# A long convolution and an MLP on one core: k transposed by DMA, q's statistics from an early copy, shorter tables, h transposed by DMA

## The chip, the cores and the metric

The kernel runs on one core of a Trainium2 chip. The metric is the device time of one execution in microseconds. The kernel before was run three times: 261.87, 262.96 and 264.95 us, so its median is 262.96 us.

## The reference

All arrays are bf16. q, k and v are 2048 x 512 (time by channel), and the filter `ssm_k` is 512 x 2048. F is 1792.

```
k_shift[s] = sum over j in 0..3 of k[s - j] * shift_k[:, j]        # four taps, zeros before the start
kv = k_shift * v
y  = irfft(rfft(kv, 4096) * rfft(ssm_k, 4096))[:2048] + kv * ssm_D   # causal convolution along time
h  = q + layernorm(q) * y
x  = layernorm(h)                                                    # the block below works on this
g  = gelu(layernorm(x) @ w1)
g  = its four channel groups shifted by -1, +1, -2, +2 time steps
x1 = x + g @ w2
out = h + x1 + gelu(layernorm(x1) @ w3) @ w4
```

## The kernel before

The long convolution is computed as a two-level Fourier transform by matmuls. A time index s is split as s = 32 n1 + n2 with n1 below 64. The k part first applies the four taps, multiplies by v and gets `kv`; the rows of `kv` then have to lie with n1 on the partitions, and so do the rows of the filter h (`Rk` and `Rh`). A first level of matmuls (`stage_a`, 16 calls for k and 16 for h) gives `Tk` and `Th`; a second (`stage_c`, 16 calls for each) gives the spectra `xt`; DVE multiplies them (`product`); two more levels go back (L647 and `last_level`). Then come the gate with layernorm(q), the layernorm of h, and the MLP with w1, w2, w3 and w4.

All work is put into one list of numbered steps (`Plan.add`). A long list of numbers written out by hand, `ISSUE`, gives the order in which they are issued; a letter behind a number names the engine for a step that more than one engine could do (A is ACT, V is DVE, G is POOL). Within an engine, and on the queue of an engine that issues DMAs, the order of the list is the order of execution. The numbers with which `add` is called are the planner's estimates; they do not act at run time. All DMAs of the kernel before are issued by SP.

These names and lines are touched by the change or by the steps of the prediction:

- k is loaded row-major, 16 consecutive time steps to a partition, with a halo of three rows (`load_k`, L211 to L215, and L226 to L229). `k_transposed` (L370 to L386) transposes it on PE in five groups, 76 transposes of 128 x 128, and ACT or DVE copies each group from PSUM to `kT`.
- `k_taps` (L390 to L406) makes the four taps by 32 matmuls against a diagonal table `dg`, eight times; DVE multiplies the result by v into one of two buffers `kvqt`.
- `k_rows` (L408 to L415) then moves each quarter of `kv` by four SBUF-to-SBUF DMAs to its place in `Rk`: n1 on the partitions, one DMA for each half of the channels and each parity of the source partition. Each of these 16 DMAs writes 64 partitions.
- `h_layout` (L418 to L432) does the same for h by transposes on PE.
- `stage_a` for k waits for all the DMAs of `k_rows`: its list of sources, L451, names every one.
- The table `Wc` for `stage_c` is made of three planes of cosines and sines, computed in two halves by POOL, DVE and ACT (L329 to L352), and spread by four DMAs (L353 to L358). The table `Wf` for the last level has a second half `Wf2`, made in the same way by POOL, DVE and ACT (L502 to L511) in the buffers `kvqt` when k is done with them.
- q is loaded once, into `q_sb`, by two DMAs of 64 partitions each (L519 to L522), after h has left that memory. Its mean and variance are taken by 16 pairs of DVE instructions (`stats`, L551 to L556), and ten small ones give the scale (L557).
- h after the gate (`hs`) is normalised to `hn` (L735 to L746) and transposed on PE (`on_pe`, L748 to L760), two tiles of 128 rows at a time, for w1. The input of w3 is transposed by DMA for three groups out of four (L860 to L863) and on PE for the first.

Of the kernel before, what the change touches and what calls it, by code (L numbers as in the profile page):

```python
# [16 lines left out]
P = 128  # L17
S = 2048
# [22 lines left out]
25 3 0 5 7 4 1 2 49 9 26 8 11 29 24 21 6 50V 31 23 13 10 51 16 85 32G 14 22 52 12 20 86V 87 48 15 19 40 74 17 98  # L41
88A 27 34 46 108 35V 99A 37 75 91 109V 53 36 89 39 92 66 76G 28 102 67 90 33 97 100 93 103 62 18 128 30 94 57G
96 47 131 68 101 133 64 38 107 134 132V 104 42 69 105 95 44 63 106 65 77 118 78V 41 79 135V 110 80 54G 83 58 84
45 59 55 112 60 43 119V 129 70 113 71 73 72 111 136 130A 81 117 82 115 122 114 212 137A 120 123 56 61 200 121
138 210 179 201A 208 211V 186 126 209A 127 196 124 187V 197A 206 125 184 116 213 207A 185V 188 214 182 189A 183V
180 139 190 181A 204 202 140G 205V 191A 155 156A 203V 153 163 154A 147 164V 173 148A 174V 151 149 152A 167 141
169 150A 168V 171 170A 177 172V 159 178A 198 160V 175 199A 157 176V 158A 161 192 223 162A 165 239 257 166A 243
194 235 258 195A 261 224 241 193A 259 245 225 142 263 244 260V 265 262A 143 240 237 266A 273 219 144G 264A 275
221 217 277 274A 267 271 276A 289 238 268 272A 287 246 270 278A 283 215 290A 269 285 229 284A 297 280 288A 279
286A 295 236 282 298A 299 281 301 296A 233 313 291 302A 307 292 300A 309 230 294 314A 311 293 308A 242 304 310A  # L50
319 303 312A 321 222 306 325 320A 305 323 231 322A 315 326A 337 316 324A 331 234 317 338A 335 318 332A 333 218
327 345 336A 328 347 334A 343 227 346A 329 349 420 330 348A 385 363 366 226 340 365 344A 339 367 364 228 342
350A 341 145 352 146 351 220 354 353 232 396 216 355 247 356 394 397A 248 358 398 249 357 395A 250 360 359 399A
390 251 400 362 368 391A 252 361 392 253 401V 414 393A 406 254 407V 416 415A 404 417A 255 405V 410 402 411A 408
256 403V 388 409A 386 389V 387A 412 379V 421 413A 380V 371V 373V 370A 418 422 369V 382A 383V 374V 384V 430 378V
423A 372V 375V 381A 424 457 431A 425 428 376A 465 432 458A 426 433 466A 492 429 434 419 500 436 435 427 437 467
377A 438 493A 501A 527 459 441A 468 442A 460 443A 445 469 444A 463 535 446A 470 471 689 464 528A 461 447 472 462
494 448A 473 536A 455 502 477A 495 476A 503 479A 480 496 453 478A 537 481A 449 498 506 454 482 504 456 483A 507
499 451 497 505 538 450 508 486 452 488 487 490 541 512A 484 539 489 511V 491 529 515 485 474 568 530 516A 569
542 531 514A 513V 533 517 532 572 534 540 518A 439 475 543 521 525 440 546A 547V 509 570 522 550 510 571 526 523  # L60
551A 549V 519 548V 575 524 552 520 577 553A 573 595 578 574 579 556 581 554 557 580 576 582 583 558 555 560 559
592 596 585A 584V 561 597 587A 588 594 615 589A 586V 593 565 590 617 618 591A 600 601 544 616 714 562 716 566
715 567 564 692 545 717 563 598 696 693 599 604 690 605 602 698 647 699 697 691 704 649 708 619 705 603 712 606
709 706 713 702 707 607V 700 620 703 608 609V 710 701 648 610 694 711 623 650 627 695 624 613A 718 719 614 653
611V 621 612 625 622 626 628 629 630 651 631 652 659 657 734 658 660 728 671 632 655 735 633 736 654 723 729 738
634 635 672 724 673 674 675 676 636 637 638 645V 639A 643V 646 739 640 737 644 750 725 752 751 677 727 678 742
679 753 680 641V 720 730 642 743 726 748 731 656 722 661 662 732 663 721 685V 749 756 686 744 733 740 687V 745
761 688 754 741 664 746 665 755 666 667 668 788 669 747 670 681V 770 762 771 789 786 763 768 787 799 778 784 779
683V 769 684 757 682 785 764 765 824 758 780 825 759 794 772 781 760 782 773 766 783 774 767 792 775 790 793 776
791 818 777 826 819 804 827 806 805 828 807 820 829 830 821 812 831 800 813 814 801 808 815 822 809 810 816 811  # L70
823 795 817 833 796 832 798 802 803 797 838 834 837 836 835 842 839 841 840 843 844 845
# [3 lines left out]
class Plan:  # L75
# [5 lines left out]
    LAT = 0.2  # L81
# [25 lines left out]
    def issue(self):  # L107
        done = set()
        for word in ISSUE.split():
            i = int(word.rstrip("AVG"))  # L110
            where, fn, deps = self.ops[i][:3]
            assert deps <= done
            done.add(i)
            if len(where) > 1:
                fn(word[-1])
            else:
                fn()
        assert len(done) == len(self.ops)
# [3 lines left out]
def kernel(  # L122
# [48 lines left out]
    slot("C", [P, 24064], "kin")  # L171
    slot("S1", [P, DC, S], "hraw")
    slot("B", [P, 11776], "kta")
    slot("A", [P, 16384], "tta")
    slot("W", [P, 3, 16, 4, N2, 4], "Wc")
    slot("S2", [P, N2, 2 * P], "Rh")
# [31 lines left out]
    def dma(us, fn, r=(), w=()):  # L208
        add({"S": us}, fn, r, w)
# [723 lines left out]
```

## Time and profile before

| | us |
|---|---|
| median of three executions | 262.96 |
| the profiled execution | 262.43 |
| its span, first to last instruction | 260.4 |
| PE busy, share of the span | 227.0, 87% |
| DVE busy | 180.7, 69% |
| ACT busy | 152.7, 59% |
| POOL busy | 30.0, 12% |
| share of PE, of DVE on the chain that ended last | 49%, 23% |
| bytes moved by DMA, mean rate | 21.15 MB, 81 GB/s |

The span is the stretch from the first to the last instruction; the execution lasts 2.0 us longer. Busy time counts a PE that executes matmuls, whether or not they follow each other at its full rate. The page cuts the span into 40 slices of 6.5 us; a digit is the busy share of an engine in a slice, in tenths. The chain is found by going back from the last instruction, at each step to what released it. A line such as L412 is a line of the kernel before. The DMA share is the mean busy share of the 16 DMA engines.

### The profile page before, as it was taken

The page shows a single profiled execution, that of the slowest core. Times are in us where ns is not written, and L with a number is a line of the kernel's source. Part 1 is how long each engine was busy: PE and PEld are TensorE (multiplying, and loading weights), DVE is VectorE, ACT ScalarE, POOL GpSimd, SP SyncE. Part 2 cuts the span into 40 slices and gives each one's busy share as a digit, 9 for nine tenths or more (in the row PEclk, how much of TensorE's full clock was granted, in tenths as well). Part 3 has the DMA queues.
Part 4 walks back from the last instruction along what each step waited for, and adds up shares of the span by engine and source line. Part 5 has one row for each costly group of instructions (what it writes and reads, how often), then busy time and mean ns, then how long its engine had stood idle before and what let it go on. Part 6 is the DMA issues. An engine that isn't in the chain of part 4 may idle for free.

```text
span 260.4 us, 4761 instructions
## 1 busy us (share of the span) xinstructions
PE 227.0 (87%) x1933; PEld 148.4 (57%) x1946; DVE 180.7 (69%) x410; ACT 152.7 (59%) x194; POOL 30.0 (12%) x37
## 2 busy tenths in 40 slices
PE   2959998989987929657699999999999999999993
PEld 2859998869987918523345454444444444444441
DVE  8895849979999999999999964897290421001341
ACT  2618158997989969999887664524163307604000
POOL 8989200303000000000000000000000000000000
PEclk9986999797999988997799999999999999999999
DMA  6986494970000079200000000020450021000141
GB/s 186 359 320 202 130 256 126 199 149 3 3 1 3 0 269 381 81 0 0 0 3 0 1 0 4 20 60 0 63 123 19 20 63 40 0 0 3 26 95 41
DMA packets 25044, 21.15 MB, mean 81 GB/s; under 512 B 14655, under 2 KB 21823, under 8 KB 24894
## 3 DMA queue, kind: packets, MB, share of 16 engines
q1 hardware_dynamic: 25022, 20.85, 28.7%
q8 instruction: 15, 0.25, 0.4%
q14 instruction: 7, 0.06, 0.1%
HBM read 13.50 MB, written 2.10 MB: 60 GB/s over the span
## 4 chain that ended last, share of the span: by engine, by line
PE 49%; DVE 23%; issue 1%; ACT 1%
PE pw L768 24%; PE p L890 18%; DVE Yp L586 7%; PE p L828 5%; DVE bst L552 3%; DVE Gs L163 2%; DVE Yp L590 2%; DVE Yp L593 2%; PE pt L756 2%; DVE qn L635 1%; DVE wts L711 1%; DVE hh L713 1%; ACT hh L740 1%; DVE mvq L553 1%; DVE xt L163 0%
## 5 line engine op out<-in xcount | busy, mean ns | idle before, releaser
L768 PE MATMUL pw<-act,wts 128*128 128x512 bf16 x285 | 65.3, 383 | 1.5 <-ACT act L161 1.3
L772 ACT ACTIVATE g<-pw 128x512 bf16<-128x512 f32 x56 | 32.5, 596 | 48.9 <-PE pw L768 48.9
L890 PE MATMUL p<-wts,g 128*128 128x512 bf16 x217 | 48.8, 379 | 0.3
L768 PEld LDWEIGHTS <-wts 128*128 128x128 bf16 x288 | 28.4, 99 | 35.4 <-issue 3.1
L895 DVE TENSOR_TENSOR wts<-p,wts 128x1024 bf16<-128x1024 f32 (+1 forms) x9 | 9.9, 1106 | 54.2 <-PE p L890 48.4
L890 PEld LDWEIGHTS <-g 128*128 128x128 bf16 x224 | 21.9, 98 | 26.4
L399 PE MATMUL psh<-kta 128*128 128x128 bf16 x256 | 17.7, 239 | 3.1 <-ACT tta L313 3.1
L586 DVE TENSOR_TENSOR Yp<-xt 128x2048 bf16<-128x2048 bf16 (+1 forms) x20 | 19.3, 999 | 0.0
L399 PEld LDWEIGHTS <-kta 128*128 128x128 bf16 x256 | 17.2, 108 | 3.3 <-issue 3.3
L161 ACT CAST xt<-pch 128x1024 bf16<-128x1024 f32 x16 | 16.1, 1041 | 2.4 <-PE pch L473 1.5
L470 PE MATMUL pck<-Tk,Wc 128*128 128x256 bf16 x64 | 16.1, 290 | 1.6 <-ACT xt L161 1.3
L472 PEld LDWEIGHTS <-Wc 128*128 128x128 bf16 x128 | 14.8, 115 | 2.8 <-issue 2.8
L161 ACT CAST xt<-pck 128x1024 bf16<-128x1024 f32 x15 | 15.2, 1034 | 1.0 <-DVE Yp L586 1.0
L834 DVE SCALAR_TENSOR_TENSOR x<-hh,rho,p 128x512 bf16<-128x512 bf16 x16 | 11.7, 739 | 5.5 <-PE p L828 5.5
L470 PE MATMUL pch<-Th,Wc 128*128 128x256 bf16 x64 | 14.7, 272 | 0.9 <-ACT xt L161 0.7
L473 PEld LDWEIGHTS <-Wc 128*128 128x128 bf16 x128 | 14.8, 115 | 0.5
L828 PE MATMUL p<-wts,act 128*128 128x512 bf16 x61 | 14.8, 379 | 0.2
L404 DVE TENSOR_TENSOR kvq<-psh,kin 128x1024 bf16<-128x1024 f32 x8 | 9.7, 1220 | 7.6 <-PE psh L399 7.6
L470 PEld LDWEIGHTS <-Wc 128*128 128x128 bf16 x128 | 14.8, 115 | 0.1
L473 PE MATMUL pck<-Tk,Wc 128*128 128x128 bf16 x64 | 14.7, 229 | 0.0
L472 PE MATMUL pck<-Tk,Wc 128*128 128x128 bf16 x64 | 14.7, 229 | 0.0
L647 PE MATMUL pg<-CSG,Yp 128*128 128x128 bf16 x128 | 9.3, 236 | 5.8 <-DVE Yp L590 5.1
(130 smaller groups left out, 407.1 us busy)
## 6 DMA issues: line engine op xcount, KB each, us to landing
wts<-in_B_w_dram SPq DMA_DIRECT2D x2, 1792.0 KB, 10.1
kin<-in_A_k_dram SPq DMA_DIRECT2D x4, 512.0 KB, 7.1
kin<-in_A_v_dram SPq DMA_DIRECT2D x4, 512.0 KB, 6.9
hraw<-in_A_ssm_k_dram SPq DMA_DIRECT2D x4, 512.0 KB, 9.0
kin<-kvq SPq DMA_DIRECT2D x16, 128.0 KB, 3.3
q_sb<-in_A_q_dram SPq DMA_DIRECT2D x2, 1024.0 KB, 10.6
out_dram<-wts SPq DMA_DIRECT2D x14, 128.0 KB, 2.3
Wc<-tta SPq DMA_DIRECT2D x4, 384.0 KB, 5.6
```

The lines of the kernel that those rows point to most:

```text
L161: A.copy(o, src)
L399: T_.matmul(pv[:, i, c * P:(c + 1) * P], lhsT=kT()[:, c, t0 + i + 3 - j, :], rhs=dg()[:, c, j, :], start=(j == 0), stop=(j == 3))
L470: T_.matmul(pv[:, kk, :, :].rearrange("p r d -> p (r d)"), lhsT=W[0], rhs=Tw.rearrange("p r d -> p (r d)"), start=True, stop=False)
L472: T_.matmul(pv[:, kk, 0, :], lhsT=W[1], rhs=Tw[:, 1, :], start=False, stop=False)
L473: T_.matmul(pv[:, kk, 1, :], lhsT=W[2], rhs=Tw[:, 0, :], start=False, stop=True)
L586: v(0.08 + 1.14 * s, lambda i=i: V.tensor_tensor(out=pr(i), in0=x(0), in1=x(1)[:, i:i + 1].to_broadcast([P, 2, n, 8]), op=MUL), ["C"] + rx ...
L768: T_.matmul(ps[:], lhsT=wt(w)[:, k, m * P:(m + 1) * P], rhs=xT()[:, k, 4 * b * P:(4 * b + 4) * P], start=(k == 0), stop=(k == DC - 1))
L772: add({"A": 0.59}, lambda: A.activation(dst(), X[pkey][:], ACT.Gelu_apprx_tanh), r + [pkey, "gelu"], [key])
L828: T_.matmul(ps[:, i, :], lhsT=gT()[:, m, t + i + 2 + off[m], :], rhs=wt("w2")[:, m, :], start=(m == 0), stop=(m == 3))
L834: v(0.74, lambda t=t, i=i, key=key: V.scalar_tensor_tensor(out=X["x1"][:, t + i, :], in0=hn()[:, t + i, :], scalar=rho[:, t + i:t + i + 1] ...
L890: T_.matmul(ps[:, i, :], lhsT=X["g2"][:, b % 2, m, s0:s0 + P], rhs=wt("w4")[:, m, :], start=(m == 0), stop=(m == FC - 1))
L895: v(0.62 * (hi - lo), lambda j=j, lo=lo, hi=hi, key=key: V.tensor_tensor(out=obb()[:, j, lo:hi], in0=X[key][:, lo:hi], in1=ofb()[:, j, lo: ...
```

## The change

1. **k channel-major by transposing DMAs.** The k loads, the 76 PE transposes and their five PSUM copies are gone. Sixteen transposing DMAs from HBM, issued by SP, write `kT` directly, with 16 zero columns ahead of it. A tile is now 128 consecutive time steps; the taps read `kT` shifted by j columns. v is loaded in the same layout (1 KB runs instead of 4 KB). In `k_rows` a tile of 128 consecutive steps covers four values of n1, so each DMA moves 128 source partitions (256 channels each) to four destination partitions with 32 values of n2 each: 32 DMAs of 64 KB instead of 16 of 128 KB.
2. **Statistics of q from a second early copy.** Eight more DMAs (64 partitions, four tiles, 256 KB each) bring q into memory that is free in the first stage, and the 16 pairs of statistics instructions read it there. They are issued among the first stage's work. `q_sb` is still loaded later, for the norm and the gate.
3. **Half of two tables by sign or exchange.** The second half of each plane of `Wc` is the first half times plus or minus one by partition (three DVE instructions in place of three ACT instructions and two on DVE or POOL). `Wf2` is `Wf` with the halves of the partitions exchanged, one of them with changed sign: one DVE instruction and four DMAs in place of iotas, phases and two sines.
4. **Transposes of h by DMA in three groups.** For the groups 1, 2 and 3 of `hn`, twelve transposing DMAs on SP take the place of six groups of eight PE transposes and six PSUM copies. Group 0 stays on PE.
5. **Queues and order.** The loads of the first stage (h, v, the early q, two small ones: 18 in all) are issued by ACT (letter Q), 13 of them ahead of its first other instruction. `ISSUE` is new as a whole. On SP stand first 12 of the k transposes, then 15 DMAs of `k_rows` mixed with the other four transposes and the four of `Wc`, then the other 17 of `k_rows`, then q. On PE all of `stage_a` for h stands ahead of `stage_a` for k.

The new `ISSUE` and the planner's estimates are left out here, and so are renamed arguments.

```
+    KT = S + 16
+    K_PE = 0
+    BY_DMA = (1, 2, 3)
...
+    def load(us, fn, r=(), w=()):
+        add({"S": us, "Q": us}, lambda e: fn(A if e == "Q" else nc.sync), r, w)
...
+    for t in range(K_PE, NT):
+        add({"T": 1.3}, lambda t=t: nc.sync.dma_start_transpose(
+            kT()[:, :, 16 + t * P:16 + (t + 1) * P], kd[t * P:(t + 1) * P, :]), ["B"], [("kT", t)])
...
+    for t0 in range(0, NT, 4):
+        for h in range(2):
+            load(0.9, lambda e, t0=t0, h=h: e.dma_start(q_part(t0, t0 + 4)[h * N1:(h + 1) * N1], qd[h, :, t0:t0 + 4, :]),
+                 r=("C" if t0 < 12 else "B",), w=[("qc", t0, h)])
...
+    def k_taps(u):
...
+                        s0 = 16 + (2 * u + i) * P - j
+                        T_.matmul(pv[:, i, c * P:(c + 1) * P], lhsT=kT()[:, c, s0:s0 + P],
                                   rhs=dg()[:, c, j, :], start=(j == 0), stop=(j == 3))
...
-    def k_rows(qr):
-        for h in range(2):
+    def k_rows(q):
+        for i in range(4):
             for g in range(2):
-                dma(0.5, lambda h=h, g=g: nc.sync.dma_start(
-                    Rk()[g * N1:(g + 1) * N1, 16 * h + 4 * qr:16 * h + 4 * qr + 4, :],
-                    kvqt[qr % 2][h:P:2, :, g * 256:(g + 1) * 256]),
+                n1 = g * N1 + 16 * q + 4 * i
+                dma(0.35, lambda e, g=g, i=i, n1=n1: e.dma_start(
+                    Rk()[n1:n1 + 4, :, :], kvqt[q % 2][:, i, g * 256:(g + 1) * 256]),
...
+    sine(1.15, lambda: plane(1, 0), u, ("u", 0), ("t", 1, 0), False)
+    cosine(1.15, lambda: plane(0, 0), u, ("u", 0), ("t", 0, 0))
+    v(0.4, lambda: V.tensor_scalar(plane(2, 0), plane(1, 0), -1.0, None, op0=MUL), ["A", ("t", 1, 0)], [("t", 2, 0)])
+    for a in range(3):
+        v(0.4, lambda a=a: V.tensor_scalar(plane(a, 1), plane(a, 0), sgnF, None, op0=MUL),
+          ["A", "pf", ("t", a, 0)], [("t", a, 1)])
...
-        stats(lambda: X["q_sb"], mvq, t, ["S1", ("q", 0), ("q", 1)], "mvq")
+        stats(lambda t: q_part(t, t + 1)[:, 0], mvq, t, ["C" if t < 12 else "B", ("qc", t - t % 4, 0), ("qc", t - t % 4, 1)], "mvq")
...
+    v(0.6, lambda: V.tensor_scalar(flat2(kvqt[1][:]), Wf[:, 0].rearrange("p n k -> p (n k)"), -1.0, None, op0=MUL),
+      wfs, [("kvq", 1, 0), ("kvq", 1, 1)])
+    for hf in range(2):
+        for h in range(2):
+            def rows(e, hf=hf, h=h):
+                x = slice(1024 * hf, 1024 * hf + 1024)
+                src = Wf[:, 0].rearrange("p n k -> p (n k)") if hf == h else flat2(kvqt[1][:])
+                e.dma_start(flat2(kvqt[0][:])[64 * h:64 * h + 64, x], src[64 - 64 * h:128 - 64 * h, x])
...
-            for i in (0, 2):
+            for i in range(4 if b in BY_DMA else 0):
+                add({"T": 1.3}, lambda t=4 * b + i: nc.sync.dma_start_transpose(
+                    xT()[:, :, t * P:(t + 1) * P], hn()[:, t, :]), ["C", "B", ("hn", 4 * b + i)], [("xT", 4 * b + i)])
+            for i in (0, 2) if b not in BY_DMA else ():
                 on_pe(lambda j, t=4 * b + i: hn()[:, t + j, :], 4 * b + i, [("hn", 4 * b + i), ("hn", 4 * b + i + 1), "B"])
```

## The prediction

> **What bounds the kernel now.** I read the page's slices first, then busy time by stage, then the chain, then each engine in order of time around the edges of the stages.
>
> ```profile
> PE   2959998989987929657699999999999999999993
> DVE  8895849979999999999999964897290421001341
> DMA  6986494970000079200000000020450021000141
> ...
> 40.50:58.70 18.20, 15.58 (x260) 13.58 (x258) 15.71 (x14) 17.09 (x19) 2.26 (x2) 0.90 0.71 154
> 58.70:66.90 8.20, 8.20 (x92) 7.72 (x92) 7.93 (x16) 6.68 (x8) 2.24 (x2) 0.81 0.01 2
> 66.90:101.00 34.10, 26.52 (x343) 25.76 (x341) 34.08 (x68) 29.67 (x32) 0.00 (x0) 0.95 0.26 90
> 127.10:260.40 133.30, 128.24 (x624) 60.09 (x636) 67.61 (x201) 55.48 (x89) 0.00 (x0) 0.99 0.13 28
> ```
>
> A window's columns are its length, then busy us and count of PE, weight loads, DVE, ACT and POOL, then granted clock, DMA share, GB/s. There are four stages. Up to 40.5 PE works through k and h. From 40.5 to 58.7 ACT and DVE copy the 32 tiles Th and Tk out of PSUM (17.1 of 18.2 us on ACT). From there to 127 DVE is full with products, norms and gates. After 127.1 PE is full to the end. Two instants tie the first two stages to the k rows:
>
> ```profile
> 36.77 8.37 SPq L412 DMA_DIRECT2D kin<-kvq  x8
> ...
> 47.48 1.67 PE L446 MATMUL pak<-WA,kin 64*128 64x128 bf16 x24 [0.42 <-ACT Th L161]
> ...
> 58.67 0.37 PE L470 MATMUL pck<-Tk,Wc 128*128 128x256 bf16 x1 [0.33 <-ACT Tk L161]
> ```
>
> SP issues the last row copy (`k_rows`) at 44.5; the first matmul on the rows is at 47.48, the first of `stage_c` at 58.67. `stage_a` for k lists every row copy as a source, so nothing of it starts before the last has landed.
>
> **The k rows decide.** Before, a row copy moves 128 KB to 64 partitions, 16 times. After, it moves 64 KB (128 rows of 512 bytes) to four neighbouring partitions, 32 times: the same 2 MB. No transfer of the trace goes to so few partitions. The nearest rows:
>
> ```profile
> 8.00:17.00 9.00, 7.29 (x106) 6.96 (x104) 7.95 (x7) 3.31 (x2) 8.91 (x8) 1.00 1.04 394
> 32.50:34.50 2.00, 2.00 (x37) 1.90 (x36) 1.24 (x2) 0.00 (x0) 0.00 (x0) 1.00 1.27 288
> 47.50:56.50 9.00, 8.17 (x133) 7.09 (x135) 8.78 (x9) 8.68 (x10) 2.07 (x2) 0.81 0.98 208
> ```
>
> The first window holds loads to 128 partitions: 394 GB/s. The third holds q's two loads, each to one half of the partitions: 208 GB/s, with the engines called busy throughout (their 16 KB packets took 1277 ns, against 159 ns for 4 KB in the first). The second holds Wc, to 32 partitions but every fourth one: 288 GB/s in 256-byte pieces. So it isn't the number of partitions that counts but how they are spread. I read this as 16 lanes of about 25 GB/s (394/16), eight partitions each, of which a contiguous half reaches eight (8 x 26 = 208). Four neighbours then reach one lane: 64 KB at 26 GB/s is 2.5 us. The two q loads write different halves and still sum to 208, so one queue's transfers follow each other and don't share the lanes.
>
> Bounds for one row copy: below, 0.33 us, the shortest plain issue on SP (a v load at 20.05; the copies of before took 0.62); above, 5.0 us, if 208 GB/s shrinks in proportion to partitions (13 GB/s). I take 2.4 us: one lane at 26 GB/s gives 2.5, and the copies of before, whose 128 KB went in 0.55 us (packet records around 43.3), give 238/8 = 30 GB/s or 2.2. [...]
>
> **The transposing DMAs for k.** Sixteen, on SP, instead of the k loads, 76 PE transposes (7.1 us: 1.89 + 4.15 + 1.07 in PE's order of time) and five PSUM copies. The twelve such DMAs of before:
>
> ```profile
> L861 SPq DMA_TRANSPOSE act<-act x12: 1189/1214/2041, 167.1 to 207.7; - x12
> ...
> DMA to landing us min/median/max: 2.3/2.4/4.6
> ```
>
> So 1.21 us of SP each; about 0.75 us of all DMA engines (512 packets of 256 bytes, 18 ns). Theirs read SBUF, the new ones HBM: bounded by 0.75 (engines alone) and 2.4 us (each waits for the one before); I take 1.21, since the issues of before stand that far apart whatever lands. Twelve stand first on SP: 0.7 + 12 x 1.21 + 1.2 to land = 16.4 us. [...]
>
> **The queue after that.** SP's new order: twelve transposes, then 15 row copies mixed with the four other transposes and the four Wc copies (1.37 us each by L354, 5.50 for 4), then 17 row copies, then q. From 16.4: 32 x 2.4 = 76.8, plus 4 x 0.75 and 4 x 1.4 = 8.6: the last lands at 101.8. The wait that this adds stands on PE in front of `stage_a` for k; behind it on PE is everything else, the h half being done by then. Then 16 tiles by two engines: before, 32 took 17.3 us (41.2 to 58.5), so 8.7, plus 0.2: `stage_c` starts at 110.7 against 58.67, **+52.0**.
>
> **Statistics of q.** 16 of 0.60 and 16 of 0.09 us on the chain, 11.0 us, leave the DVE stage. Seven stood before 63.3, when DVE had nothing else. Nine are left, 5.4, and the aggregates, 1.3: 6.7 us. What is late next is ACT: 31 casts `xt`, 0.91 to 0.97 us apart, are some 29.5 of the 34.1 us, and the products wait for them. I take **-5** (0 to -6.7). In the front they lie beside 30 of 40.5 busy us of DVE, and in the wait above for certain; without that cover they cost up to 11. The second copy is 2 MB more in a DMA share of 0.79 (0 to 40.5): eight transfers at 208 GB/s, 10 us beside the first transposes; if these get half of the engines, up to 8 us, kept for the range. Its issues go to ACT with all loads, 18 of 0.33 to 0.73 us: ACT is busy for 18.4 of 40.5 us, so nothing; if not covered, 9.
>
> **Tables.** Three trigonometric ACT instructions of 1.15 us go and 1.7 us of DVE come; Wf's second half was made on POOL, DVE and ACT beside the DVE stage (2.3 us on ACT) and becomes 0.6 us of DVE and four DMAs, needed only after 107.8. Nothing, or -2.
>
> **Transposes of h.** Six groups of eight leave PE's full stage: 1.03 + 0.46 + 0.45 + 0.53 + 0.45 + 0.45 = 3.4 us. Twelve DMAs come. For the first group, `hn` ends at 126.3 to 128.5 on ACT; SP issues at 126.3 and then every 1.21, the last at 129.9, landed at 132.3. PE covers it until 130.5 with 16 matmuls of w1; 1.8 us are lost. Later groups have w2 and w1 (3.5 us each) as cover; without it each would lose the same. Net **-1.5** (0 to -3.4).
>
> **Sum.** 262.4 (the profiled execution, 260.4 of span and 2.0 around it; the median shown is 263.0) + 52.0 - 5 - 1.5 = **308**. With 2.2 to 2.6 us a copy and the bounds above, its own range is 298 to 316.
>
> **Rivals.**
> 1. *The copies overlap or aren't limited by a lane* (faster). SP's issue then sets the end: 16 x 1.21 + 4 x 1.37 + 32 x 0.45 and 0.7 give 40, landed by 43; taps end at 36, the h half of `stage_a` at 44.4, `stage_c` starts at 53.3, -5.4. With -5 and -1.5: 250.5; at 0.6 us an issue, 255. Speaks for it: packets of before, 27 ns for 512 bytes, ran at up to 300 GB/s inside a burst, over 208, so there is some buffer; 64 KB may fit. It decides below about 0.75 us a copy. I say 253; chance 0.28.
> 2. *Four engines, no lane limit*: 128 packets of 27 ns on four engines are 0.86 us; two lanes, 1.25. Copies 27.5 to 40 us: landed at 52.5 to 65, `stage_c` 61.4 to 74, +2.7 to +15.3, less 6.5: 259 to 271, and some 5 more if those engines' share of the loads lies in front; 266. [...] Chance 0.14.
> 3. *The transposes don't do what they should*: from HBM at 2.4 us each they end at 39 and not at 20, and with free copies the front is 14 us later than in rival 1: 265. Speaks against it: the L861 issues are 1.21 apart while landing takes 2.4. Chance 0.08.
>
> **How the numbers follow.** Serial copies 0.50. Faster by over 1%: rival 1, 0.28. Within 1% (about what a measurement of this kernel tells from no change; its three runs spread by 1.2%): 0.03 each of rivals 2 and 3. Slower: 0.50 + 0.11 + 0.05 = 0.66. The range must hold rival 1's bulk too: 250 to 316; likeliest case alone 298 to 316.
>
> **What would show it.** Right: row copies that land ever later after their issue, a gap on PE of tens of us in front of `pak`, ended by a DMA of `kin<-kvq`, DMA share low in it, and products 3.6 to 3.9 us apart afterwards. Wrong: the last copy landed by 45 and `pck` starting by 56, or k transposes more than 1.3 us apart.

## The result

The changed kernel takes 318.43 us (median of four executions, 317.41 to 319.86), the kernel before 262.56 us (four executions on the same chip): 1.211 times as long, with a 95% interval of 1.202 to 1.220. The prediction was 308 with a range up to 316. The sign came out as predicted and the cause in part; several terms of the sum did not, and the time lies 2.4 us above the range. Of all the executions below, one is left out of its median because it was in a slower state of the chip (268.01 us, of the kernel before with the transposes of h by DMA).

The profiled execution took 317.41 us, with a span of 315.6. Its slices, to be read beside those of the kernel before:

```profile
PE   0704940405191399995874579899999999999994
DVE  8109800302473299999999999789585413301051
DMA  8899989793632923003930033200201404002012
```

A digit stands for a slice of 7.9 us here. The first fifteen slices, up to `stage_c` at 116.6 us, are a front in which PE and DVE mostly wait (each is busy for 47 us of it); what follows looks like the kernel before from its tenth slice on. The time by stage, as windows (length, then busy us and count of PE, weight loads, DVE, ACT, POOL, then granted clock, DMA share, GB/s):

```profile
0.00:31.77 31.77, 10.22 (x128) 9.81 (x129) 15.90 (x31) 8.46 (x7) 16.76 (x26) 0.79 0.99 222
31.77:116.59 84.82, 37.47 (x513) 34.72 (x513) 31.42 (x45) 23.25 (x25) 5.58 (x6) 0.64 0.69 85
...
116.59:146.00 29.41, 28.82 (x385) 28.43 (x384) 28.52 (x43) 27.66 (x30) 0.00 (x0) 1.00 0.09 20
146.00:162.00 16.00, 9.65 (x129) 8.59 (x128) 15.57 (x35) 12.09 (x14) 0.00 (x0) 0.89 0.86 296
162.00:181.50 19.50, 10.77 (x78) 5.58 (x79) 18.67 (x59) 18.39 (x24) 0.00 (x0) 0.84 0.02 4
181.50:315.60 134.10, 125.60 (x580) 56.93 (x592) 67.83 (x197) 51.95 (x87) 0.00 (x0) 1.00 0.19 39
```

The cuts are: the first row copy, the first matmul of `stage_c`, the end of its last one, the first `py` (a matmul of `last_level`), the first matmul of w1. Before, `stage_c` started at 58.7; now at 116.6. That is +57.9 us in the front. From there to the end it is 199.0 us against 201.7, so -2.7. Both together give the 55.2 by which the span grew.

The queue of SP and the first matmuls on the rows (start, duration, line and operation; in brackets the idle time before and what ended it):

```profile
0.73 16.34 SPq L235 DMA_TRANSPOSE kta<-in_A_k_dram  x12
31.77 1.37 SPq L411 DMA_DIRECT2D kin<-kvq  x2
...
78.78 22.23 SPq L411 DMA_DIRECT2D kin<-kvq  x17
...
107.60 0.87 PE L444 MATMUL pak<-WA,kin 64*128 64x128 bf16 x8 [11.43 <-DMA kin<-kvq]
116.59 0.28 PE L468 MATMUL pch<-Th,Wc 128*128 128x256 bf16 x1
```

The issue of the twelve transposes took 16.3 us; 14.5 (12 x 1.21) were predicted. But the first row copy follows at 31.8 and not at 16.4, the last seventeen only from 78.8 on, and `stage_a` for k starts at 107.6, released by a row copy. Why they are issued so late stands on DVE:

```profile
23.94 2.45 DVE L368 TENSOR_SCALAR tta<-tta,pf 128x1024 bf16<-128x1024 bf16 x1 [14.62 <-ACT tta L327]
30.54 1.20 DVE L402 TENSOR_TENSOR kvq<-psh,kin 128x1024 bf16<-128x1024 f32 x1
...
56.92 0.20 DVE L323 TENSOR_SCALAR tta<-tta 128x64 int32<-128x64 int32 x1 [18.66 <-DMA Wc<-tta]
72.62 0.69 DVE L323 TENSOR_SCALAR tta<-tta 128x1024 int32<-128x1024 int32 x1 [12.59 <-DMA Wc<-tta]
83.58 0.69 DVE L323 TENSOR_SCALAR tta<-tta 128x1024 int32<-128x1024 int32 x1 [9.04 <-DMA Wc<-tta]
```

DVE multiplies by v (L402) in the order of the list. The first multiply stands behind steps that wait for ACT's first sines, until 23.9. Ahead of three later multiplies stands a step of the phases, L323, that writes the tile `tta`; and the four copies `Wc`, which stand ahead of it in the list, read that tile, though other columns of it. So DVE waits until a `Wc` copy has landed, 18.7 + 12.6 + 9.0 = 40.3 us in all. Those copies stand on SP behind row copies, land 10.0, 6.1, 9.7 and 9.1 us after their issue starts, and the row copies behind them need the next multiply. In the trace of the kernel before, no instruction of DVE or POOL waits for a `Wc` copy.

A second coupling is in the compiled program. The transfers of both queues take eight DMA semaphores in turn, in the order of the program; each waits on its semaphore until the transfer eight places earlier has landed. The records of the trace name the semaphores, 100 to 107: ACT's fourth load, issued at 8.9, waits on 104, which belongs to the transpose that SP issued at 4.9 and that landed at 8.88. In the kernel before, all transfers are on one queue and in one order. Now loads on ACT's queue wait for transfers of SP's: ACT issues three loads at once and the fourth at 8.9, the thirteenth at 20.7, and its first other work starts at 21.4.

### The profile page after: what moved, and what is told of

The parts are those of the page before. It is cut to its first block, busy times and chain, and to the rows that moved or that the text cites. A ratio compares the mean times of both kernels' runs of the same rounds, so it can differ in the third digit from the quotient of the medians.

```text
span 315.6 us, 4558 instructions
## 1 busy us (share of the span) xinstructions
PE 222.5 (71%) x1810; PEld 144.1 (46%) x1822; DVE 177.9 (56%) x404; ACT 141.8 (45%) x184; POOL 22.3 (7%) x32
## 4 chain that ended last, share of the span: by engine, by line
PE 46%; DMA 18%; SPq 14%; DVE 12%; ACT 5%; issue 3%; POOLq 1%; ACTq 1%; POOL 0%; DVEq 0%
PE pw L785 18%; PE p L910 15%; DMA Wc<-tta 9%; SPq L235 7%; SPq L411 6%; DVE bst L537 4%; DMA wts<-in_B_w_dram 4%; DMA kin<-kvq 2%; PE p L848 2%; PE pch L468 2%; PE pck L468 2%; DMA act<-hh 2%; DVE hh L730 2%; DVE wts L728 2%; ACT xt L162 2%
## 5 line engine op out<-in xcount | busy, mean ns | idle before, releaser
L785 PE MATMUL pw<-act,wts 128*128 128x512 bf16 x280 | 64.0, 380 | 4.0 <-DMA act<-hh 3.5
L789 ACT ACTIVATE g<-pw 128x512 bf16<-128x512 f32 x56 | 32.2, 597 | 50.5 <-PE pw L785 50.5
L398 PE MATMUL psh<-kta 128*128 128x128 bf16 x256 | 24.1, 282 | 40.8 <-DVE kvq L402 31.2
L398 PEld LDWEIGHTS <-kta 128*128 128x128 bf16 x256 | 23.3, 132 | 41.4 <-issue 27.1
L910 PEld LDWEIGHTS <-g 128*128 128x128 bf16 x224 | 21.9, 98 | 26.4
L323 DVE TENSOR_SCALAR tta<-tta 128x1024 int32<-128x1024 int32 (+3 forms) x6 | 2.6, 428 | 40.3 <-DMA Wc<-tta 40.3
L599 DVE TENSOR_TENSOR Yp<-xt 128x2048 bf16<-128x2048 bf16 (+1 forms) x20 | 19.5, 1006 | 0.5 <-ACT xt L162 0.2
L444 PE MATMUL pak<-WA,kin 64*128 64x128 bf16 x128 | 8.5, 289 | 11.8 <-DMA kin<-kvq 11.4
L162 ACT CAST Th<-pah 128x1024 bf16<-128x1024 f32 x10 | 9.7, 1023 | 14.6 <-PE pah L444 14.6
L164 DVE CAST Tk<-pak 128x1024 bf16<-128x1024 f32 x8 | 9.4, 1210 | 11.4 <-PE pak L444 11.4
L470 PEld LDWEIGHTS <-Wc 128*128 128x128 bf16 x128 | 14.5, 113 | 0.8 <-issue 0.8
L468 PE MATMUL pck<-Tk,Wc 128*128 128x256 bf16 x64 | 14.7, 272 | 0.0
L468 PEld LDWEIGHTS <-Wc 128*128 128x128 bf16 x128 | 14.5, 113 | 0.1
L425 PE MATMUL pt<-ident,hraw 128*64 128x128 bf16 x128 | 8.1, 313 | 9.2 <-POOL hraw L503 7.6
```

Source lines behind the costliest of these rows:

```text
L162: A.copy(o, src)
L398: T_.matmul(pv[:, i, c * P:(c + 1) * P], lhsT=kT()[:, c, s0:s0 + P], rhs=dg()[:, c, j, :], start=(j == 0), stop=(j == 3))
L468: T_.matmul(pv[:, kk, :, :].rearrange("p r d -> p (r d)"), lhsT=W[0], rhs=Tw.rearrange("p r d -> p (r d)"), start=True, stop=False)
L470: T_.matmul(pv[:, kk, 0, :], lhsT=W[1], rhs=Tw[:, 1, :], start=False, stop=False)
L599: v(0.08 + 1.14 * s, lambda i=i: V.tensor_tensor(out=pr(i), in0=x(0), in1=x(1)[:, i:i + 1].to_broadcast([P, 2, n, 8]), op=MUL), ["C"] + rx ...
L785: T_.matmul(ps[:], lhsT=wt(w)[:, k, m * P:(m + 1) * P], rhs=xT()[:, k, 4 * b * P:(4 * b + 4) * P], start=(k == 0), stop=(k == DC - 1))
```

## Experiments

Three theories were set against each other. **Partitions**: the copies into four neighbouring partitions are too slow, whatever their order. **Order**: the two couplings above hold the copies back. **Front**: the transposes of k and the early loads are too much beside each other, whatever the copies do. In each run the start of `stage_c` is the first number to look at, since 198 to 200 us of the span follow it in all of those that change the front.

### Partitions and order, one at a time

**Four partitions, spaced by four.** Nothing else changes but the table of `stage_a` for k, made by some ten small instructions more.

```
-                n1 = g * N1 + 16 * q + 4 * i
+                n1 = g * N1 + 16 * q + i
...
-                    Rk()[n1:n1 + 4, :, :], kvqt[q % 2][:, i, g * 256:(g + 1) * 256]),
+                    Rk()[n1:n1 + 13:4, :, :], kvqt[q % 2][:, i, g * 256:(g + 1) * 256]),
...
-                              rhs=WA[g * N1:(g + 1) * N1, :, :].rearrange("p a b -> p (a b)"),
+                              rhs=(WAk if w == "k" else WA)[g * N1:(g + 1) * N1, :, :].rearrange("p a b -> p (a b)"),
```

> The four partitions that one row copy writes stand four apart instead of side by side (the order of the 16 n1 of a group is permuted, and k's table for stage_a with it, by some ten small instructions more); all else and the order of issue stay. Theory A, the copies: four neighbouring partitions share one way into SBUF, which alone takes some 21 GB/s (3 us a copy). Spread, a copy that runs alone takes under 1.3 us, the 17 that stand queued from 78.8 to 101 land by about 92, the Wc copies in between take less than half of their 10 us, and stage_c starts near 90 instead of 116.6: 292 us (280 to 305). Theory B, the order: the rows are late because DVE and POOL wait in order behind ACT's loads and behind the Wc copies, and a copy has four DMA engines whatever its partitions are: a lone copy stays near 3 us, stage_c starts between 112 and 118, 317 us (312 to 321).

Measured: 290.03 us, 1.107 (1.099 to 1.115) of the kernel before. In its order of time:

```profile
60.80 12.72 SPq L432 DMA_DIRECT2D kin<-kvq  x17
...
79.81 0.88 PE L465 MATMUL pak<-WAk,kin 64*128 64x128 bf16 x8 [6.32 <-DMA kin<-kvq]
88.79 0.27 PE L489 MATMUL pch<-Th,Wc 128*128 128x256 bf16 x1
```

The same seventeen copies are issued within 12.7 us instead of 22.2 (in each, the second waits for a multiply of DVE; the sixteen from there on take 10.4 instead of 15.5 us), and `stage_c` starts 27.8 us earlier, as the theory of the partitions had said (near 90). DVE's stops behind `Wc` shrink with it, from 40.3 to 17.1 us in the table of waits, though their order is unchanged: most of what looked like a fault of order was the same slow copies, seen from DVE. The packet records show the rates. With neighbouring partitions, the queue of seventeen starts at some 60 packets of 512 bytes per us (88 to 90 us) and rises to 158 (100 to 102); spaced, it holds some 164 per us from 65 to 76 us, 84 GB/s.

**`Wc` behind the phases.** 85 to 88 are the four copies.

```
-73G 88 184 74 105 66G 113 150 75 107 76 85 120 77
+73G 184 74 105 66G 113 150 75 107 76 120 77
...
-176 153A 71 116
+176 153A 71 88 85 86 87 116
```

> The order of issue alone: the four Wc copies stand behind all phases and sines that write the same tile, so that nothing on DVE or POOL waits for one of them to land. Theory B (order): DVE's three stops before L323, 18.7 + 12.6 + 9.0 us between 38 and 84, go; the multiplies of kv end near 50 and the row copies are all issued by 70; what is left is their own rate, 0.8 to 2.4 us for each of some 28 that are left at 40, so the last lands between 65 and 100 and stage_c starts between 74 and 109: 296 us (275 to 310). Theory A (the copies' rate sets the end, whenever they are issued): no change within 5 us, 314 to 321.

Measured: 309.89 us, 1.184 (1.176 to 1.192); `stage_c` at 109.3. The three stops of DVE are gone, but the copies were not issued by 70:

```profile
41.34 13.33 SPq L409 DMA_DIRECT2D kin<-kvq  x8
...
72.47 21.48 SPq L409 DMA_DIRECT2D kin<-kvq  x17
```

Eight copies need 13.3 us of issue and seventeen 21.5, 1.3 to 1.7 us each, where single row copies of the changed kernel are issued in 0.55 (from 85.5 to 88.4 us). The order is worth 8.5 us here, not the 22 that I had put down, and the copies' own rate holds the rest.

**Phases and first sines ahead of ACT's loads.**

```
-36Q 48 39Q 50 45 26Q 32Q 7Q
+36Q 48 50 45 51V 40 52 42 78 79 80 39Q 26Q 32Q 7Q
```

> The order of issue alone: the first phases, the table load for Sin and the first sines stand ahead of all but three of ACT's loads. Theory: ACT's first compute at 21.4 was late because its loads, thirteen of them, each wait on a DMA semaphore for the landing of the eighth DMA before; DVE stands behind those sines until 23.9 and the first multiply of kv at 30.5. With the sines early DVE runs on from about 10, and the first row copy is issued at 18 to 22 instead of 31.8. The Wc copies still stop DVE three times, so of these 11 us only a part reaches stage_c: it starts 4 to 11 us earlier, 310 us (305 to 315). Rival: the transposes or the loads of k, and not ACT, set the first kv; then the first row copy stays after 29 and the time between 315 and 321.

Measured: 319.06 us, 1.216 (1.206 to 1.226): no change, so the rival holds. DVE, no longer behind ACT, now waits until 22.5 for a load of q, and the first multiply for v itself; the first row copy starts at 29.0:

```profile
22.48 1.29 DVE L535 BATCH_NORM_STATS2 bst<-kin 128x6 f32<-128x512 bf16 x2 [12.31 <-DMA kin<-in_A_q_dram]
...
27.75 1.22 DVE L400 TENSOR_TENSOR kvq<-psh,kin 128x1024 bf16<-128x1024 f32 x1 [0.75 <-DMA kin<-in_A_v_dram]
```

**Both orders**, with the copies as they were:

> Both orders together, the copies unchanged. If the order is the whole cause (copies at 0.8 us when several are queued): the row copies start at 20, are all issued by 50, landed by 55, stage_c starts near 64: 262 us (255 to 270). If the copies' way into SBUF is serial at 2.4 us, as predicted: 32 of them from 20 end at 97 to 105, stage_c starts at 106 to 114, 305 to 314. Between the two, lone copies at 3 us and queued ones at 0.8: 280 to 300; 285 is my value.

Measured: 311.71 us, 1.190 (1.182 to 1.198); `stage_c` at 111.9. That is the upper case of the three, though the copies do not all take 2.4 us: the first starts at 29.2, not 20, and the rest runs at 1.3 to 1.7 us a copy with the four `Wc` copies between.

### The copies by themselves

A kernel that only copies; after each group one DVE instruction reads from all of it, so its idle time is the time from the first issue to the last landing.

```
+    copies(1, lambda j: (0, 4, 1))
+    copies(8, lambda j: (0, 4, 1))
+    copies(8, lambda j: (8 * j, 8 * j + 4, 1))
+    copies(8, lambda j: (4 * (j % 2), 4 * (j % 2) + 4, 1))
+    copies(1, lambda j: (0, 13, 4))
+    copies(8, lambda j: (0, 13, 4))
...
+    copies(1, lambda j: (0, 97, 32))
+    copies(8, lambda j: (0, 97, 32))
```

> No computation at all: only copies of 64 KB in 512-byte pieces from 128 partitions into 4, one by one or 8 in a row, each group waited for before the next, and some of 128 KB into 64 partitions as before has them. Theory (one way into SBUF for neighbouring partitions, 27 to 28 GB/s, shared by the four engines of a copy): 8 copies to partitions 0 to 3 take 18.8 us and more (2.35 each); 8 copies to eight groups of four that stand 8 apart start at the same rate and rise as the four engines drift apart, 8 to 17 us; spaced by 4, 8 or 32, 8 copies take 6.2 us (0.78 each, four engines at 27 ns a piece). Rival (the engines of a copy, not its partitions, set the rate): the same time within 20% for all groups of 8 to four partitions. The 128 KB copies: 0.55 us each.

The lines of DVE in order of time, for the groups of the diff and the two of 128 KB copies at the end:

```profile
44.15 0.17 DVE L78 COPY seen<-R 128x8 bf16<-128x8 bf16 x1 [4.27 <-DMA R<-src]
68.75 0.17 DVE L78 COPY seen<-R 128x8 bf16<-128x8 bf16 x1 [24.43 <-DMA R<-src]
82.17 0.17 DVE L78 COPY seen<-R 128x8 bf16<-128x8 bf16 x1 [13.25 <-DMA R<-src]
97.11 0.17 DVE L78 COPY seen<-R 128x8 bf16<-128x8 bf16 x1 [14.77 <-DMA R<-src]
99.80 0.17 DVE L78 COPY seen<-R 128x8 bf16<-128x8 bf16 x1 [2.52 <-DMA R<-src]
108.23 0.17 DVE L78 COPY seen<-R 128x8 bf16<-128x8 bf16 x1 [8.26 <-DMA R<-src]
...
122.65 0.17 DVE L78 COPY seen<-R 128x8 bf16<-128x8 bf16 x1 [2.97 <-DMA R<-src]
135.70 0.17 DVE L78 COPY seen<-R 128x8 bf16<-128x8 bf16 x1 [12.88 <-DMA R<-src]
...
150.87 0.17 DVE L78 COPY seen<-R 128x8 bf16<-128x8 bf16 x1 [2.88 <-DMA R<-src]
160.15 0.17 DVE L78 COPY seen<-R 128x8 bf16<-128x8 bf16 x1 [9.10 <-DMA R<-src]
```

The last column gives the price of a further copy, (eight minus one) / 7:

| four partitions | one, us | eight, us | each further, us |
|---|---|---|---|
| 0 to 3, always | 4.27 | 24.43 | 2.88 |
| 0 to 3 and 4 to 7 in turn | 4.27 | 14.77 | 1.50 |
| eight groups of four, 8 apart | 4.27 | 13.25 | 1.28 |
| 0, 4, 8, 12 | 2.52 | 8.26 | 0.82 |
| 0, 32, 64, 96 | 2.97 | 12.88 | 1.42 |
| 64 partitions, 128 KB | 2.88 | 9.10 | 0.89 |

(For the second and third row the single copy is that of the first.) Four neighbours take 2.88 us for 64 KB, 22.8 GB/s, and the same bytes into 0, 4, 8, 12 take 0.82. The rival, that only the four engines of a copy count, had wanted all rows within 20%; it falls. What is left of it is the floor of 0.82 us: 32 packets of 27 ns one after the other on each of four engines would be 0.86, an estimate. The 27 ns are the median of the 512-byte packets in the kernel before. The four are read from the changed kernel's records: a row copy lands in four parts there (101 counts four from 44.18 to 44.25), a `Wc` copy in 16, and from 88 to 102 us 4.3 to 5.1 packets of row copies are under way at a time. The theory missed one row too: it had put 0, 32, 64, 96 at 0.78 like the other spaced ones. Its 27 to 28 GB/s lay among the rates of the first bursts of row copies in the changed kernel (26.0 to 32.2 GB/s, from 34 to 70 us); into 0 to 3 alone 22.8 was measured.

The copies that hold each other up are those into the same four neighbours, and not into the same eight as the prediction had read it: 4 to 7 beside 0 to 3 nearly halves the price (1.50 us against 2.88), while 0, 32, 64, 96, four partitions far apart, cost half of 0 to 3 (1.42) and more than 0, 4, 8, 12 (0.82). Why the far ones cost more than the near ones with a distance of four, no run shows.

So the prediction's 2.4 us came near for copies into one group (2.88), but not for the queue: the queue's copies go to different groups, and several are under way at once (in the changed kernel seven are issued from 85.5 on, the last of them at 89.7, before the first of them has landed at 90.28). Row three, 1.28 us, is the nearest to the changed kernel, whose copies also go to different groups, but in the order of its list (partitions 84, 100, 108, 40 and so on at the start of the seventeen) and not 8 apart.

### The rest: 24 us with the copies spread

**Spread and both orders.**

> Spread partitions and both changes of order together. Theory: with the copies at 0.78 us queued, they no longer hold anything, and the order counts: DVE's three stops behind the Wc copies, 6.2 + 6.2 + 4.7 = 17 us in the run with spread partitions alone, go, and stage_c starts at 70 to 76 instead of 88.8: 274 us (268 to 280). Rival: what the order frees is taken by the next limit in the front (v and q land at 30 and later, the last four transposes of k stand behind row copies on SP): 284 to 291.

Measured: 286.30 us, 1.095 (1.090 to 1.099); `stage_c` at 86.1. The rival holds: the order was worth 3.7 us once the copies were faster.

**And all transposes of k ahead of the first row copy.**

> Spread partitions, both changes of order, and the last four transposes of k ahead of the first row copy on SP's queue. In the run without this they were issued at 29.8, 38.0, 46.4 and 57.1, each behind row copies that wait for kv, and the last taps and 17 row copies waited for them until 58.9. Theory: with kT whole by 25, only the row copies' own rate (0.78 us), the four Wc copies and the taps are left: rows landed by 60 to 66, stage_c starts at 68 to 75 instead of 86.1: 270 us (266 to 277). Rival: v and q land at 28 to 40 and set the multiplies of kv; then stage_c starts at 78 to 86 and the time is 278 to 286.

Measured: 287.35 us, 1.095 (1.090 to 1.101); `stage_c` at 85.8. Again the rival: v is issued only between 26.4 and 31.6, behind the transposes and the early loads of q in the turn of the semaphores. Its loads in this run, and in the next one without q's early copy:

```profile
26.36 0.37 ACTq L218 DMA_DIRECT2D kin<-in_A_v_dram  x1
...
31.58 0.51 ACTq L218 DMA_DIRECT2D kin<-in_A_v_dram  x1
```

```profile
19.02 0.94 ACTq L218 DMA_DIRECT2D kin<-in_A_v_dram  x2
...
29.73 0.46 ACTq L218 DMA_DIRECT2D kin<-in_A_v_dram  x1
```

**Without the early copy of q.**

```
-            load(0.9, lambda e, t0=t0, h=h: e.dma_start(q_part(t0, t0 + 4)[h * N1:(h + 1) * N1], qd[h, :, t0:t0 + 4, :]),
-                 r=("C" if t0 < 12 else "B",), w=[("qc", t0, h)])
+            load(0.9, lambda e: None, w=[("qc", t0, h)])
```

> The same without the early copy of q: its eight loads are left out, and the statistics, as many as before, are taken of a constant tile (q's own statistics are not computed). Theory: v's loads are issued 8 places earlier and don't share the queue with 2 MB that arrive at half rate, so v lands some 8 to 10 us earlier and stage_c starts 5 to 10 us earlier than with the copy. Rival: the loads lie beside the transposes of k anyway: within 2 us.

Measured: 280.48 us, 1.071 (1.065 to 1.077); `stage_c` at 79.8. So the early copy costs 6.0 us of front and 6.9 in all, with all that waits for its loads.

**With a quarter of its bytes.**

> The same with the eight early loads of q, but each a quarter of its bytes (the statistics are taken four times of the same row, so q's own are not computed). It tells bytes from places: if the wait of each load for the eighth DMA before it is what counts, stage_c starts where it does with the whole copy (within 3 us); if the bytes count, where it does without the copy.

Measured: 282.87 us, 1.078 (1.072 to 1.085); `stage_c` at 82.9, halfway. Three quarters of the bytes are worth 2.9 us. The other 3.1 are the rest of the bytes, the eight places in the turn, and a third cause that these runs don't separate: the statistics stand ahead of multiplies in DVE's order, and DVE waits for a load of q until 27.3 with the whole copy and until 24.6 with a quarter of it, while without it the statistics wait for no load.

**Rows as before.** The transposes stay, but the taps read every sixteenth column, so that the rows go in 16 copies of 128 KB to 64 partitions.

```
-                        s0 = 16 + (2 * u + i) * P - j
-                        T_.matmul(pv[:, i, c * P:(c + 1) * P], lhsT=kT()[:, c, s0:s0 + P],
+                        s0 = 16 + 2 * u + i - j
+                        T_.matmul(pv[:, i, c * P:(c + 1) * P], lhsT=kT()[:, c, s0:s0 + (P - 1) * NT + 1:NT],
...
+                    Rk()[g * N1:(g + 1) * N1, 16 * h + 4 * q:16 * h + 4 * q + 4, :],
+                    kvqt[q % 2][h:P:2, :, g * 256:(g + 1) * 256]),
```

> The transposes of k by DMA stay, but the taps read every 16th column of kT, so that the rows of kv lie as before: 16 row copies of 128 KB to 64 partitions instead of 32 of 64 KB to four. Order as in the run with both orders, all taps after all 16 transposes. It also says what the rest of the change is worth. If the layout of the copies is what the change lost: the row copies are done by 50, stage_c starts at 57 to 64, 256 to 264 us; my value 261. If the front is late for other reasons (2 MB more of loads, transposes beside loads, ACT behind its loads): stage_c starts after 66, 265 to 280.

Measured: 291.04 us, 1.112 (1.107 to 1.117); `stage_c` at 90.5, although the copies were as before: outside both ranges. In my order the loads of h took turns with the transposes: its first half was used at 30.6, its second at 43.9, and PE stood behind it.

**Two reordered fronts**, the first with 32 spread copies, the second with 16 of 128 KB:

> Spread partitions, and the whole front ordered anew, with the same transfers: loads of h and v between the transposes of k, one of each in turn, all sixteen transposes first on SP, the early loads of q behind the layout of h, its statistics behind the multiplies of kv, Wc behind the phases. Theory (the front is late because of the order in which the eight DMA semaphores come round, not because of the bytes): v and h are there by 16, kT by 24, the row copies run from 22 at 0.78 us with 6 to 8 us of Wc between, are landed by 56, stage_c starts at 65 to 70 instead of 85.8: 267 us (263 to 272). Rival (the bytes: transposes, loads, q and rows together fill the queue): stage_c starts at 76 or later, 278 to 286.

> The same order with the rows of kv laid out as before (taps on every 16th column of kT): 16 row copies of 128 KB to 64 partitions instead of 32 of 64 KB to four; all layouts of h ahead of the taps on PE. Beside the run with 32 spread copies it tells what is left of the copies' price: if the four engines of a copy are what remains, rows are landed by 48, stage_c starts at 57 to 62, 256 to 262 us; if the transposes of k and the added loads set the front, stage_c starts within 4 us of the other run.

Both missed: 295.08 us (1.128, 1.119 to 1.136; `stage_c` at 94.0) and 299.70 (1.148, 1.139 to 1.157; 98.8). I had put q's early loads behind the layout of h, and they took turns on the semaphores with row copies. Fourteen row copies were issued over 31.9 us. Six went by 33.8; the other eight, whose multiplies were done by 38.6, stood until 44.9 behind the turn of loads of q that ACT issued only from 39.9 on:

```profile
22.55 31.93 SPq L430 DMA_DIRECT2D kin<-kvq  x14
```

They say nothing of the copies' engines, but they show the turn of eight semaphores at its worst.

**Transposes alone.** Rows as before, no early copy of q, all loads and transposes on one queue in the order of need; in the second run the statistics stand among DVE's first instructions instead of in one block.

> What the transposes of k cost by themselves: rows laid out as before (16 copies of 128 KB to 64 partitions), no early copy of q (the statistics are taken of a constant tile, so q's own are not computed), all loads and transposes on SP's queue in the order in which they are needed (h, v, then four transposes to each further load). Theory (transposes and loads fit beside each other if no load waits for a later transfer): h is there by 8, kT by 28, taps end by 45, rows are landed by 50, stage_c starts at 58 to 64: 255 to 262 us, as before or a little less. Rival (sixteen transposes at 1.27 us, 21 us in which the loads make little way, are too much for the front whatever the order): stage_c starts at 70 or later, over 267 us.

> As the run before, but the 16 statistics (of the constant tile; q's own are not computed) stand among the first instructions of DVE, where it waits for the transposes, and not in one block of 11 us ahead of the casts of Th. Theory (the transposes and the loads beside them set the front: k is whole at 30, PE has done 4 us of work by then where the kernel before has done 21): only that block goes, stage_c starts at 72 to 75 instead of 83.9, 273 us (270 to 276), still slower than before by 3 to 5%. Rival (the block was hidden beside the copies): stage_c stays at 80 or later.

Measured: 284.66 us (1.087, 1.079 to 1.094; `stage_c` at 83.9), and 277.63 (1.057, 1.054 to 1.060; `stage_c` at 75.8). The theory of the first run fell and its rival held. In the second run the block was worth 8 us, as the theory had it, though the run ended 0.8 and 1.6 us above its two ranges. Without the four-partition copies and the early copy of q the front is still 17.2 us late. The first 30 us, of this run and then of the kernel before:

```profile
0.00:30.00 30.00, 3.85 (x64) 3.66 (x64) 19.64 (x57) 8.56 (x7) 19.70 (x30) 1.00 0.98 210
```

```profile
0.00:30.00 30.00, 21.22 (x278) 20.45 (x279) 23.86 (x37) 12.72 (x12) 25.48 (x33) 0.89 0.75 250
```

PE has done 3.9 us of work where it had done 21.2, and the DMA engines are busy (0.98). Sixteen transposes, 1.26 us apart, share it with the loads; the last lands at 30.2. The 76 PE transposes that they replace took 7.1 us of PE. In this run the taps wait for all sixteen, because they read every sixteenth column; a front that starts them earlier may lose less, and was not tried without the four-partition copies. Not all of the 17.2 us need be theirs: SP issues the `Wc` copies behind eight row copies, from 45.4 on, and the first casts of `Th`, which take over the memory that these copies read, wait for them:

```profile
58.53 3.76 ACT L160 CAST Th<-pah 128x1024 bf16<-128x1024 f32 x4 [5.75 <-DMA Wc<-tta]
```

The chain that ended last goes through this wait. An earlier place for `Wc` could have brought up to 5.8 us of the 17.2; it was not tried.

### Two parts on the kernel before

**Transposes of h by DMA, alone.**

```
+            for i in range(4 if b else 0):
+                add({"T": 1.3}, lambda t=4 * b + i: nc.sync.dma_start_transpose(
+                    xT()[:, :, t * P:(t + 1) * P], hn()[:, t, :]), ["C", "B", ("hn", 4 * b + i)], [("xT", 4 * b + i)])
```

> The kernel before with one part of the change: the transposes of h of groups 1 to 3 by twelve DMAs instead of 48 on PE. Predicted for this part: -1.5 us (0 to -3.4), so 260.4 beside 261.9. If the DMAs' landing (2.4 us) is not covered in each group: 0 to +3.

Measured: 265.04 us (five executions), 1.013 (1.009 to 1.018): 3.4 us slower, not 1.5 faster. Of the table of waits (engine, line, released by; us, times, longest):

```profile
PE pw L768 <- DMA act<-hh: 4.5, 3, 3.6
```

Each group waits for its transposes, the first 3.6 us; 1.8 was predicted for the first and none for the others. The 3.4 us of PE work that went are less than these 4.5; the difference is 1.1 us. The granted clock goes the same way: 0.87 from 124.3 to 150, against 0.93 from 124.5 to 150 in the kernel before (0.97 against 0.99 from 124.5 to 257). That is some 1.5 us, an estimate (0.06 of 25.7 us). Whether the waits bring the lower clock is not shown, and the rest is not explained.

**Statistics of q left out.**

```
+        if key == "mvq":
+            v(0.1, lambda: V.memset(bst[:, t, :], 0.5), r, [("bst", t)], lat=0.08)
+            v(0.1, lambda: V.memset(mv[:, t, :], 0.5), [("bst", t)], [(key, t)], lat=0.12)
+            return
```

> The kernel before, in its own order, with the 16 statistics of q and their aggregates replaced by two small writes each (0.1 instead of 0.6 us; q's mean and variance are not computed). It bounds what moving the statistics out of the stage of products can bring. Predicted: nine of them lie on DVE's path there: -5 us (0 to -6.7), with ACT's casts late next, so 257. In the trace of after, stage_c took 4.2 us less but the stage of gates 2.8 more; if the gates lose it whatever the order, the time here is 260 to 262.

Measured: 259.60 us, 0.991 (0.988 to 0.995): -2.3 us by the means, about half of the -5. In the profiled execution the first matmul of w1 starts 4.2 us earlier (120.3 against 124.5), and from there to the end it takes 0.8 more (136.7 against 135.9). Of the 4.2, 1.1 lie ahead of `stage_c` (57.5 against 58.7), where nothing was changed; the run above starts it at 57.4 too, so this part comes from the execution and not from the statistics. The tables were not tried alone.

## Why the prediction was right and wrong

- **"The k rows decide"** was right: `stage_a` for k is released by the last row copy, at 107.6, and `stage_c` starts 9.0 us later (8.9 predicted). The reason, copies into neighbouring partitions that hold each other up, was right for about half: spacing the partitions alone takes 28.4 us off the time, and 27.8 of the 57.9 by which the front grew. The other half has the causes below.
- **"2.4 us" a copy, one after the other**: a size that was off, and in two ways. For copies into one group it is 2.88 us. But "one queue's transfers follow each other and don't share the lanes" fell: copies into different groups overlap, and a mix costs 1.28 by itself and 1.3 to 1.7 in the kernel. It had been read from two loads of 1 MB, which don't tell what copies of 64 KB do. 32 of them are 41 to 54 us, not 76.8. The 16 lanes of eight partitions were an estimate from 394 and 208 GB/s, and no run shows such a lane: copies to 0 to 3 and 4 to 7 in turn, one lane by it, cost 1.50 us each, against 2.88 to 0 to 3 alone. The 0.55 us for a 128 KB copy of the kernel before are 0.66 in its packet records (256 packets of 512 bytes from 43.16 on), by which the 2.2 us would have been 2.6.
- **"Twelve stand first on SP ... 16.4 us"**: the transposes were nearly right (16.3 us of issue against 14.5, the median 1.27 against 1.21). The step from there to the first row copy failed: it came at 31.8. "ACT is busy for 18.4 of 40.5 us, so nothing; if not covered, 9" had counted the issue time of the loads and not what they wait for. Putting compute ahead of them gains nothing, so it isn't ACT alone that is late but v and q; the early copy of q, put at "up to 8 us, kept for the range", is 6.0 us of front once the other causes are out of the way.
- **Not foreseen**: the waits of DVE for `Wc` copies. I had looked for new waits on PE, and not at which steps the new order puts behind a copy that reads their tile. Worth 8.5 us in the changed kernel, 40.3 of idle time on DVE.
- These errors nearly cancel: the copies are 23 to 36 us cheaper than predicted and start 15.4 later, with DVE's stops between. `stage_c` starts at 116.6 against 110.7 predicted, +5.9. That the front came so near was luck: the terms that failed are the price of the copies in a row (76.8, in place of 41 to 54) and the waits in front of and between them, which the sum had at nothing.
- **Statistics, "-5"**: mis-sized. `stage_c` did become 3.3 us shorter (32.7 to 29.4), but the gates took 2.8 more (16.7 to 19.5, with ACT at 18.4 of them); left out altogether the statistics are worth 2.3.
- **Transposes of h, "-1.5"**: wrong in sign, +3.4 by themselves. The cover that w1 was to give did not reach: SP's transposes start when `hn` is there, and that is when PE needs them. In the changed kernel PE waits 3.5 us for them, and what follows the first matmul of w1 is still 1.8 us shorter (134.1 against 135.9), at a granted clock of 1.00 against 0.99; what they are worth there was not measured alone.
- **Behind `stage_c`**, -6.5 was predicted in all and -2.7 measured: another +3.8. With the +5.9 that is 9.7, and 307.9 + 9.7 = 317.6 against 317.4 of the profiled execution.
- **The rivals.** Rival 1 gave 253 with copies that cost nothing. Kernels close to that case take 277.6 (rows as before, no early q) to 290 (spread): its front of 53 us left out what the transposes and the early loads do to each other. Rival 3, "the transposes don't do what they should", is thus part of the truth, by another way than 2.4 us each. Rival 2's four engines are the floor of 0.82 us; no row of the kernel before shows that number (its row copies land in 16 parts), the changed kernel's copies, which land in four, do.

What stays open: how the 17 us of the second run of the transposes alone divide between the transposes' own time on the queue, the taps that wait for all of them and the wait for `Wc`, and what the two shorter tables bring.

No version tried beats the kernel before with all of its work done.

## What to carry to other kernels

Before splitting a copy into more and smaller ones, look at which partitions each one writes: bytes per copy fell by half here and the time for all of them rose, because each had four neighbours (16 of 0.89 us, against 32 of 1.28, in the kernel that only copies). Take a tile's reader into account when its writers are reordered, also when it is a DMA of other columns. And cost a load by where it comes in the turn of the DMA semaphores, not by its issue: in these programs a load that stands eight places behind a slow transfer waits for it, on whichever queue (ACT's fourth load here until 8.9).

## What the runs showed that was not expected

- Copies into the same four neighbouring partitions are the dearest (2.88 us for 64 KB). Distance alone does not make them cheap: 0, 32, 64, 96 cost 1.42, while 0, 4, 8, 12 cost 0.82.
- Copies of one queue into different groups overlap: two groups in turn 1.50 us each, against 2.88 into one.
- A lone copy into four neighbours lands 1.75 us later than one spread by four (4.27 against 2.52).
- With spread copies, the order of the same steps and transfers alone moved the time from 286 to 295 us.
